# One set of split weights for both parts of an expert, and six experts in the order of their counts

## The chip, the cores and the metric

The kernel runs on one core of a Trainium2 chip. The metric is the device time of one execution in microseconds, as a median of the runs. TensorE is called PE here, VectorE DVE, ScalarE ACT, GpSimd POOL and SyncE SP, as in the profile.

## The reference

```
# q, k, v, a_re, a_im: (4, 8, 768, 48); S_re, S_im start at zero
for t in range(768):                       # gated linear attention
    S_re, S_im = ar*S_re - ai*S_im + k_t v_t^T, ar*S_im + ai*S_re
    y[t] = q_t @ S_re
x = y as (3072, 384)
noisy = x @ w_gate + log1p(exp(x @ w_noise)) * noise     # 8 experts
top2, softmax over the two
out[r] = sum over the two of  wt * (relu(x[r] @ w1[e]) @ w2[e])   # 384x1024, 1024x384
h = max(max(out @ u1, out @ u2), out @ u3)               # 384x768
return h @ w_out                                         # 768x384
```

With 3072 tokens and two experts each, 6144 rows fall on eight experts: 768 on average, and the counts are known only when the kernel runs.

## The kernel before

The work has four stages. **Attention**: 24 chunks of 128 tokens, four batches of six chunks. The k-th chunks of the four batches make a level, so there are six levels, and the state (`mb`) of each batch goes from level to level: it is added to (L777) and multiplied by the decay `lx` (L783). `chunk` (L695) and `gates` (L456) write the steps of a chunk. **Routing**: `route` (L822) takes two chunks at a time, twelve times in all. It finds the two experts of each token and the row that the token gets in each (PE's L882 to L886, DVE's L866 to L900), and `scatter` (L937, issued by POOL, L940) writes the token's row, split into two f16 halves, into `xs_rows`, where each expert has its own 3072 rows. **Experts**: relu(x w1) w2 with every operand split into two f16 halves, so that three matmuls stand for one. **Final stage**: `hidden` and `last` (L1541 to L1586) gather the two results of each token from `ys_rows` and compute the three products, their maximum and the last product.

An expert is computed in two parts. `first_pass(e)` takes its first 384 rows (RA), `second_pass(n)` the next 432 (RB), 816 in all (CAP). Rows beyond that go through a loop behind the experts, which is skipped where no expert has that many. A part is: rows of `xs_rows` loaded with a transpose (L1006, six transfers), 72 matmuls into eight tiles of h (L1037, in the second pass L1098), relu and its low half on ACT and DVE (L437; L1046, L1107), 72 matmuls back (L1057, L1124; of 432 rows, 48 make a tile of their own in 24 short matmuls, L1131), eviction to `ya` (L443, L1144) and its writing to `ys_rows` (L1069, L1152). A first pass writes its rows to `yf_rows` as well.

`weigh` (L1008) brings an expert's weights: seven pieces, each loaded by SP into one of four buffers `wst` (L997), then split by ACT (high half, L985) and DVE (low half, L987). Each expert has its weights loaded and split for both passes, but for the expert that is last of the first passes and first of the second ones: 15 sets of 7 pieces.

`bump` sees to it that the first 384 rows of an expert are full before the attention's last chunks are routed; the first passes thus need only the rows routed by then. `weigh_u` prepares the weights of the final stage: 15 pieces `raw`, three operations of DVE each into `ua` (L1177, L1182, L1186) and a split.

All steps up to the final stage are recorded as operations with their dependences, tiles and a key (place, name); a planner lists them engine by engine as the program is built, with a table of numbers by name, `P["o"]`, that sets which comes first. Each engine then runs its list in that order. Ten or so names in the table belong to the experts: `xw`, `xx`, `x1`, `xe`, `x2`, `xo` for first passes, the ones with y for second passes. SP issues nearly all transfers, in order, so a transfer that waits holds those behind it.

Of the kernel before, what the change touches and what calls it, by code (L numbers as in the profile page):

```python
# [35 lines left out]
    o=dict(load=-278.44, e1=-80.82, g=-44.76, ex=27.33, lam=13.6, t1=124.93, t2=491.73, f=-344.44, sin=58.57,  # L36
           tc=-621.27, qkv=204.29, v=669.22, a0=-227.64, a=84.82, b=-227.33, d=-609.19, c=-58.23, s=-165.23,
           l=90.33, f_=14.8, rt=-247.65, scat=-246.48, zf=803.51, gate=-153.95, noise=149.71, xw=125.96, xx=-312.17,
           x1=-201.57, xe=-424.5, x2=17.72, xo=-1189.75, yw=61.09, yx=-118.02, y1=-594.47, ye=185.57, y2=-134.08,
           yo=454.95, uw=1011.11, ue=388.46, pl=276.27, z=-83.6, mr=971.2),  # L40
# [208 lines left out]
def tile_kernel(ctx, tc, q, k, v, a_re, a_im, w_gate, w_noise, noise, w1, w2,  # L249
# [20 lines left out]

    xs = nc.dram_tensor("xs_rows", (E * NT, 2 * HD), F16).ap()

    NX = -(-((E - 2) * RA - (E * CAP - 2 * NT)) // 128) * 128
# [5 lines left out]
    zs = nc.dram_tensor("z_rows", (NT, 2 * HD), F16).ap()  # L279

# [93 lines left out]
    more = const.tile([128, E], F32, name="more")  # L374
# [630 lines left out]
    def load_rows(e, t, lo, hi, j):  # L1005
        return nc.sync.dma_start_transpose(t[:, j, :hi - lo], xs[e * NT + lo:e * NT + hi, j * 128:(j + 1) * 128])  # L1006
# [10 lines left out]
    def first_pass(e):  # L1017
        def pr(x):
            return NA + 1.5 * e, x

        weigh(e, "w1", "w2", e, pr("xw"), [("sl", ends[GA - 2], None)])
        for k in range(KD):
            for z in range(2):
                def f_x(e_, j=z * KD + k):
                    ins = load_rows(e, tl("xa", e), 0, RA, j)
                    for o in later:
                        tc.declare_no_dep(ins.ins, o.ins, reason="the second pass's rows begin after the first's")
                    loads.append(ins)
                load(f_x, pr("xx"), [("xa", e, (k, z))], xfer=0.65,
                     r=[("xs", i, None) for i in range(NA)], row="xa")  # L1030
        for f in range(KF):
            b = ("g", (e, 1, f))
# [599 lines left out]
```

## Time and profile before

| | us |
|---|---|
| median of 3 runs (978.99 to 984.77) | 984.25 |
| profiled execution: span from the first to the last instruction | 983.5 |
| PE busy (95%) | 930.6 |
| PE's weight loads busy (60%) | 586.8 |
| DVE busy (58%) | 574.0 |
| ACT busy (48%) | 476.0 |
| POOL busy (14%) | 139.0 |

The profile gives no time of that execution outside its span, so sums are made against the span. Its mean granted clock on PE is 0.979 of full speed. The transfers move 150.98 MB. A share is a mean over stages that differ: the stretches show which engine is full where.

### The profile page before, as it was taken

How to read it: one execution, taken by the hardware profiler on the slowest of the kernel's cores; microseconds unless marked ns; L12 is line 12 of the kernel's file. 1: busy time of each engine (PE TensorE's matmuls, PEld its weight loads, DVE VectorE, ACT ScalarE, POOL GpSimd, SP SyncE). 2: the span in 40 equal slices, each digit the busy share in tenths (PEclk: the TensorE clock that was granted, in tenths of full speed). 3: DMA queues.
4: the chain of work that ended last, by engine and by line, in shares of the span. 5: the costliest groups of instructions: out<-in, count | busy, mean ns of one | idle time of the engine just before them, and what ended most of it. 6: DMA issues, size and time to landing. Idle time of an engine off the chain costs nothing. (4 is left out here: it accounts for less than half of the span.)

```text
span 983.5 us, 16814 instructions
## 1 busy us (share of the span) xinstructions
PE 930.6 (95%) x6312; PEld 586.8 (60%) x6312; DVE 574.0 (58%) x1252; ACT 476.0 (48%) x922; POOL 139.0 (14%) x197
## 2 busy tenths in 40 slices
PE   3989778899999999899999999999799999999998
PEld 1868667787666766455555555555675445454544
DVE  5989748999655756565887764454344332424231
ACT  7998748978644556243445444333233132313221
POOL 0101442422001000520100000000433030300000
PEclk9999969999999999899999999999999999999999
DMA  9999848796765546379888785552335141502000
GB/s 150 211 214 271 195 120 159 182 194 165 191 185 168 158 153 201 123 223 312 253 253 238 209 208 155 147 141 79 107 116 142 40 133 36 140 25 78 25 9 33
DMA packets 247902, 150.98 MB, mean 154 GB/s; under 512 B 196488, under 2 KB 235528, under 8 KB 247816
## 3 DMA queue, kind: packets, MB, share of 16 engines
q1 hardware_dynamic: 241672, 130.98, 52.1%
q0 software_dynamic: 6144, 18.88, 6.4%
q8 instruction: 50, 0.82, 0.4%
q14 instruction: 36, 0.29, 0.1%
HBM read 89.78 MB, written 45.81 MB: 138 GB/s over the span
## 5 line engine op out<-in xcount | busy, mean ns | idle before, releaser
L437 ACT ACTIVATE hh<-bk 128x384 f16<-128x384 f32 (+1 forms) x128 | 64.6, 508 | 85.4 <-PE bk L1098 43.2
L985 ACT ACTIVATE w<-wst 128x768 f16<-128x768 f32 (+1 forms) x77 | 71.1, 932 | 59.6 <-PE bk L1057 23.3
L1057 PE MATMUL bk<-w,hh 128*128 128x384 f16 x576 | 98.6, 331 | 1.3 <-issue 1.3
L1037 PE MATMUL bk<-xa,w 128*128 128x384 f16 x576 | 99.6, 326 | 0.0
L987 DVE SCALAR_TENSOR_TENSOR w<-wst,w 128x768 f16<-128x768 f32 (+1 forms) x77 | 81.4, 1068 | 12.4 <-ACT w L985 11.5
L1571 ACT ACTIVATE th<-mx 128x512 f16<-128x512 f32 (+1 forms) x42 | 23.8, 568 | 127.2 <-DVE mx L1570 125.5
L1057 PEld LDWEIGHTS <-hh 128*128 128x128 f16 x576 | 56.7, 99 | 41.6 <-issue 6.5
L1124 PEld LDWEIGHTS <-hh 128*128 128x128 f16 x576 | 55.0, 98 | 40.3 <-issue 5.0
L1037 PEld LDWEIGHTS <-w 128*128 128x128 f16 x576 | 55.1, 98 | 34.4 <-issue 1.4
L1569 DVE TENSOR_TENSOR mx<-mx,u 128x512 f32<-128x512 f32 (+1 forms) x42 | 25.6, 610 | 62.5 <-PE u L1557 62.5
L1507 POOL DMA_INDIRECT yg<-ys_rows,sy x42 | 43.5, 1036 | 119.6 <-ACT za L1511 104.4
L940 POOL DMA_INDIRECT xs_rows<-xhl,sl x48 | 55.4, 1154 | 35.5 <-issue 18.5
L443 DVE COPY ya<-bk 128x384 f32<-128x384 f32 x37 | 20.6, 558 | 67.7 <-PE bk L1057 45.7
L732 PE MATMUL sc<-qt,kt 96*128 96x128 f32 x384 | 55.4, 287 | 4.5 <-issue 1.8
L732 PEld LDWEIGHTS sc<-qt,kt 96*128 96x128 f32 x384 | 49.3, 197 | 12.1 <-issue 4.1
L1098 PE MATMUL bk<-xa,w1b 128*128 128x432 f16 x288 | 53.2, 346 | 0.0
L1098 PE MATMUL bk<-xa,w 128*128 128x432 f16 x288 | 53.2, 346 | 0.0
L1107 DVE SCALAR_TENSOR_TENSOR hh<-bk,hh 128x432 f16<-128x432 f32 x64 | 37.9, 605 | 24.9 <-ACT hh L437 24.8
L1124 PE MATMUL bk<-w2b,hh 128*128 128x384 f16 x288 | 48.4, 326 | 0.0
L1124 PE MATMUL bk<-w,hh 128*128 128x384 f16 x288 | 48.4, 326 | 0.0
L1570 DVE TENSOR_TENSOR mx<-mx,u 128x512 f32<-128x512 f32 (+1 forms) x42 | 25.7, 611 | 37.4 <-PE u L1557 33.2
L1513 DVE SCALAR_TENSOR_TENSOR z<-yg,wt,za 128x384 f32<-128x384 f32 x22 | 12.8, 614 | 58.7 <-ACT za L1511 52.2
(204 smaller groups left out, 2012.7 us busy)
## 6 DMA issues: line engine op xcount, KB each, us to landing
wst<-in_moe_w_dram SPq DMA_DIRECT2D x45, 512.0 KB
wst<-in_moe_w_dram SPq DMA_DIRECT2D x60, 384.0 KB
xs_rows<-wst SPq DMA_DIRECT2D x8, 1152.0 KB
ys_rows<-ya SPq DMA_DIRECT2D x48, 192.0 KB
raw<-in_moe_w_dram SPq DMA_DIRECT2D x9, 768.0 KB
ar<-in_a_re_dram SPq DMA_DIRECT2D x24, 192.0 KB
ai<-in_a_im_dram SPq DMA_DIRECT2D x24, 192.0 KB
q<-in_q_dram SPq DMA_DIRECT2D x24, 192.0 KB
```

What stands on the lines that cost most here:

```text
L437: nc.scalar.activation(o, i, f, **kw)
L732: nc.tensor.matmul(tl("sc", (i, g))[:, j, :], tl("kt", i)[:, h, :], tl("qt", i)[:, h, :], start=True, stop=True)
L940: ins = nc.gpsimd.indirect_dma_start(out=xs, out_offset=bass.IndirectOffsetOnAxis(ap=sl[:, i, t:t + 1], axis=0), in_=tl("xhl", i), in_offs ...
L985: nc.scalar.activation(hi, src, AF.Copy, scale=scale)
L987: nc.vector.scalar_tensor_tensor(lo, src, scale, hi, op0=OP.mult, op1=OP.subtract)
L1037: nc.tensor.matmul(tl(*b)[:, :RA], tl("w1", e)[:, w, k, f * 128:(f + 1) * 128], tl("xa", e)[:, x + k, :RA], start=(k == m == 0), stop=(k = ...
L1057: nc.tensor.matmul(tl(*b)[:, :HD], tl("hh", e)[:, a, f, t * 128:(t + 1) * 128], tl("w2", e)[:, w, f], start=(f == m == 0), stop=(f == KF - ...
L1098: nc.tensor.matmul(tl(*b)[:, :RB], tl(n1, inst)[:, w, k, f * 128:(f + 1) * 128], tl("xa", xi)[:, x + k], start=(k == m == 0), stop=(k == K ...
L1107: nc.vector.scalar_tensor_tensor(tl("hh", xi)[:, 1, f], tl(*b)[:, :RB], 0.0, tl("hh", xi)[:, 0, f], op0=OP.max, op1=OP.subtract)
L1124: nc.tensor.matmul(tl(*b)[:, :HD], tl("hh", xi)[:, a, f, ts_], tl(n2, inst)[:, w, f], start=(f == m == 0), stop=(f == KF - 1 and m == 2))
L1507: nc.gpsimd.indirect_dma_start(out=y, out_offset=None, in_=src, in_offset=bass.IndirectOffsetOnAxis(ap=row[:, i, s:s + 1], axis=0))
L1570: nc.vector.tensor_tensor(a, a, ps[2], op=OP.max)
```

## The change

- The functions `first_pass` and `second_pass` become one, `expert(n, part, at, fresh)`. Only experts 0 and 1 have an early part (NF = 2), which takes rows from the chunks routed early; `bump` fills their first 384 rows alone.
- The parts come in a fixed order: expert 0's first, expert 1's first and second, then both parts of each of six experts one after the other, then expert 0's second. Weights are loaded and split once for both parts, but twice for expert 0: 9 sets of 7 pieces.
- The six are not experts 2 to 7 by number but by rank of their counts. DVE computes the ranks after the last route (`p_1`), SP loads the six numbers into registers (`p_er`), and the transfers of weights and rows take the expert from a register (`of`). The row limits by rank are 816, 784 and four times 768; a part of 400 or 432 rows has a tile of 16 or 48 rows, one of 384 has none. The loop for rows beyond takes the limit of each expert.
- Rows that a lower limit leaves unwritten are written once (`f_n`), fewer rows of zeros are needed, and the table `P["o"]` is a new one in all its numbers, so that the order on every engine changes.

```
-    o=dict(load=-278.44, e1=-80.82, g=-44.76, ex=27.33, lam=13.6, t1=124.93, t2=491.73, f=-344.44, sin=58.57,
...
+    o=dict(a=1637.24, a0=879.39, b=-18448.79, c=-886.02, d=-34103.66, e1=-2857.66, er=1057.34, ex=4707.9, f=-2809.26,
...
+    NF = 2
+    CAPS = [CAP] * NF + [816, 784, 768, 768, 768, 768]
...
+    xs3, ys3, yf3 = (x.rearrange("(e r) d -> e r d", e=E) for x in (xs, ys[:E * CAP], yf))
+    ER = {}
+    def of(n):
+        return slice(n, n + 1) if n < NF else bass.ds(ER[n], 1)
...
-                                         src[e][k * 128:(k + n) * 128].rearrange("(k p) f -> p k f", p=128))
+                                         src[of(e), k * 128:(k + n) * 128].rearrange("o (k p) f -> p (o k) f", p=128))
...
-    def first_pass(e):
+    def expert(n, part, at, fresh):
+        lo = RA * part
+        rows = CAPS[n] - RA if part else RA
+        early = n < NF and not part
+        inst = (n, part) if fresh else (n, 0)
...
+        if fresh:
+            weigh(n, n1, n2, inst, (NA + 1.5 * at, "xw") if early else (NI + at, "yw"),
+                  [("sl", ends[GA - 2], None)] if early else ([("er", n, None)] if n >= NF else []) + ([("swap", 0, None)] if swapped else []))
...
+            load(lambda e_, f_o=f_o: f_o(e_, ys3), pr("xo"), [("ys", xi, t)], xfer=0.6, r=[y + (None,)])
+            if part and t == nt - 1 and CAPS[n] < CAP:
+                def f_n(e_, y=y):
+                    nc.sync.dma_start(ys3[of(n), CAPS[n]:].rearrange("o n d -> (o n) d"), tl(*y)[:CAP - CAPS[n]])
+                load(f_n, pr("xo"), [("ys", xi, "no")], xfer=0.3, r=[y + (None,)])
+            if not part:
+                load(lambda e_, f_o=f_o: f_o(e_, yf3), pr("xo"), [("yf", n, t)], xfer=0.6, r=[y + (None,)])
...
+            key, rank, c2 = Q["key"], Q["rank"], Q["ohr"].rearrange("p (a b) -> p a b", b=E)
+            nc.vector.scalar_tensor_tensor(key, cnt, float(2 * E), iota8, op0=OP.mult, op1=OP.subtract)
+            nc.vector.memset(key[:, 0:NF], -1.0)
...
+        def p_er(n):
+            def f(e_):
+                ER[n] = nc.values_load(Q["ordi"][0:1, n - NF:n - NF + 1], engines=[mybir.EngineType.SP], min_val=0, max_val=E - 1,
...
-    for e in range(E):
-        first_pass(e)
...
-    for n in range(E):
-        second_pass(n)
...
+    parts = [(0, 0, True), (1, 0, True), (1, 1, False)] + [(n, part, not part) for n in range(NF, E) for part in range(2)] + [(0, 1, True)]
+    for at, (n, part, fresh) in enumerate(parts):
+        expert(n, part, at, fresh)
```

The new table moves steps of the attention too. The first place is PE at the last of the twelve routes. Before (`w_1952` is an expert's w1, seventh of eight first passes):

```order
L1037 MATMUL bk_249<-xa_2146,w_1952 128x384
L882 LDWEIGHTS tri_103
L882 MATMUL ps_389<-a_139,tri_103 128x16
L886 LDWEIGHTS ones_105
L886 MATMUL ps_389<-acc,ones_105 128x8
```

After (`w_2699` is expert 0's w2, `hh_2906` its h; the rows of the route have other lines):

```order
L1091 MATMUL bk_227<-w_2699,hh_2906 128x384
L892 LDWEIGHTS tri_103
L892 MATMUL ps_389<-a_139,tri_103 128x16
L896 LDWEIGHTS ones_105
L896 MATMUL ps_389<-acc,ones_105 128x8
```

What stays behind the route is the rest of the same part, then whole parts; what stood ahead of it changes from more than six first passes to one half of one.

The second place is POOL at the first scatters, which wait in turn for a route; `mb_113` to `mb_116` are the four batches' states. Before, twelve scatters (each with its spacer) stand in a row from the last row here on:

```order
L783 TENSOR_TENSOR mb_115<-mb_115,lx_801 96x8x48
L783 TENSOR_TENSOR mb_116<-mb_116,lx_801 96x8x48
L870 TENSOR_TENSOR acc<-acc,a_139 128x8 x4
L783 TENSOR_TENSOR mb_114<-mb_114,lx_1292 96x8x48
L939 MEMSET spacer 1x1
L940 DMA xs_rows<-xhl_501,sl 24576x768
```

After:

```order
L949 MEMSET spacer 1x1
L950 DMA xs_rows<-xhl_601,sl 24576x768
L949 MEMSET spacer 1x1
L950 DMA xs_rows<-xhl_601,sl 24576x768
L793 TENSOR_TENSOR mb_114<-mb_114,lx_1286 96x8x48
L793 TENSOR_TENSOR mb_115<-mb_115,lx_1286 96x8x48
L793 TENSOR_TENSOR mb_116<-mb_116,lx_1286 96x8x48
L949 MEMSET spacer 1x1
L950 DMA xs_rows<-xhl_640,sl 24576x768
L949 MEMSET spacer 1x1
L950 DMA xs_rows<-xhl_640,sl 24576x768
```

The decays of three states now stand behind the fourth scatter; eight scatters follow them. In all, the 20 decays stand on POOL, where before 11 did and 9 on DVE.

The third place is SP after the last route. Before, in a second pass (weights `wst`, rows `xa`, results `ya`):

```order
L1006 DMA_TRANSPOSE xa_2544<-xs_rows 128x432
L997 DMA wst_1803<-in_moe_w_dram 128x1024
L1174 DMA raw_4809<-in_moe_w_dram 128x1536
L1006 DMA_TRANSPOSE xa_2544<-xs_rows 128x432
L997 DMA wst_1853<-in_moe_w_dram 128x2x384
L1006 DMA_TRANSPOSE xa_2544<-xs_rows 128x432
```

After, where the registers and the first weights of the first expert by rank stand:

```order
L1429 DMA ys_rows<-wst_2402 128x3x384
L1261 TENSOR_LOAD ordi
L1016 DMA_TRANSPOSE xa_2583<-xs_rows 128x432
L1007 ISA
L1007 DMA wst_160<-in_moe_w_dram 128x1024
L1261 TENSOR_LOAD ordi x4
L1016 DMA_TRANSPOSE xa_2583<-xs_rows 128x432
L1261 TENSOR_LOAD ordi
L1148 DMA raw_3608<-in_moe_w_dram 128x1536
L1007 ISA
L1007 DMA wst_2279<-in_moe_w_dram 128x1024
```

Each transfer whose expert is in a register has one more instruction (ISA) ahead of it; the transposes of expert 1's second part (`xa_2583`) stand between.

## Rows read from the trace of the kernel before

**Rows 1.** Stretches: us, busy us (instructions) of PE, PEld, DVE, ACT, POOL, PEclk, DMA, GB/s.

```profile
62.00:104.00 42.00, 39.43 (x399) 34.25 (x398) 36.56 (x111) 37.78 (x86) 5.81 (x9) 0.96 1.08 236
104.00:163.00 59.00, 47.98 (x400) 40.01 (x400) 39.29 (x123) 39.06 (x88) 22.65 (x38) 0.83 0.65 153
163.00:205.00 42.00, 35.88 (x349) 31.08 (x348) 41.22 (x112) 38.72 (x83) 17.96 (x20) 0.96 0.79 179
...
432.00:687.00 255.00, 255.00 (x1576) 142.86 (x1575) 159.74 (x237) 105.49 (x167) 10.08 (x14) 1.00 0.68 199
```

**Rows 2.** PE in order of time (start us, us, line, what, count) at three places.

```profile
207.37 1.15 PE L1037 MATMUL bk<-xa,w 128*128 128x384 f16 x6
...
431.68 0.17 PE L882 MATMUL ps<-a,tri 128*128 128x16 f16 x1 [0.86 <-DVE a L866]
...
688.81 0.39 PE L1557 MATMUL u<-ua,u1h 128*128 128x256 f16 x2 [0.65 <-DVE ya L443]
```

**Rows 3.** PE in order of time, 445 to 512 us.

```profile
445.94 11.86 PE L1037 MATMUL bk<-xa,w 128*128 128x384 f16 x72
457.64 12.01 PE L1057 MATMUL bk<-w,hh 128*128 128x384 f16 x72
469.49 13.30 PE L1098 MATMUL bk<-xa,w 128*128 128x432 f16 x72
482.73 1.16 PE L1131 MATMUL bk<-w,hh 128*48 128x384 f16 x12
...
496.72 13.30 PE L1098 MATMUL bk<-xa,w1b 128*128 128x432 f16 x72
```

**Rows 4.** DVE by line; then the spread of two lines (min/median/max ns, first and last start).

```profile
L987 DVE SCALAR_TENSOR_TENSOR w<-wst,w 128x768 f16<-128x768 f32 (+1 forms) x77 | 81.4, 1068 | 12.4 <-ACT w L985 11.5
...
L783 DVE TENSOR_TENSOR mb<-mb,lx 96x384 f32<-96x384 f32 x9 | 6.9, 772 | 0.0
...
L1182 DVE SCALAR_TENSOR_TENSOR ua<-raw,ua x15: 541/950/960, 452.1 to 573.5; 128x768 int32<-128x768 int32 x9, 128x384 int32<-128x384 int32 x6
...
L783 POOL TENSOR_TENSOR mb<-mb,lx x11: 839/856/3901, 68.9 to 304.4; 96x384 f32<-96x384 f32 x11
```

**Rows 5.** DVE in order of time: the first L649 of a level.

```profile
62.35 0.55 DVE L649 SCALAR_TENSOR_TENSOR tn<-tn,bk 128x384 f32<-128x384 f32 x1
...
103.81 0.55 DVE L649 SCALAR_TENSOR_TENSOR tn<-tn,bk 128x384 f32<-128x384 f32 x1
...
161.82 0.55 DVE L649 SCALAR_TENSOR_TENSOR tn<-tn,bk 128x384 f32<-128x384 f32 x1
...
205.34 0.55 DVE L649 SCALAR_TENSOR_TENSOR tn<-tn,bk 128x384 f32<-128x384 f32 x1 [0.22 <-ACT tn L437]
```

**Rows 6.** POOL, DVE and PE in order of time, around the scatters.

```profile
109.55 3.90 POOL L783 TENSOR_TENSOR mb<-mb,lx 96x384 f32<-96x384 f32 x1 [11.61 <-DVE lx L613]
...
114.96 1.16 POOL L940 DMA_INDIRECT xs_rows<-xhl,sl  x1 [1.48 <-issue]
...
129.46 0.96 POOL L940 DMA_INDIRECT xs_rows<-xhl,sl  x1 [0.22 <-issue]
...
122.30 0.34 PE L753 MATMUL py<-qt,mb 96*64 96x128 f32 x2 [1.08 <-issue]
...
132.48 0.55 DVE L777 TENSOR_TENSOR mb<-mb,ps 96x384 f32<-96x384 f32 x1 [8.84 <-remote]
...
405.34 0.27 PE L753 MATMUL py<-qt,mb 96*64 96x128 f32 x1 [1.10 <-issue]
```

**Rows 7.** The tile nbi (min/median/max ns); then SP's queue in order of time.

```profile
L1444 SPq TENSOR_LOAD <-nbi x1: 538/538/538, 689.7 to 689.7; - x1
...
494.00 0.43 SPq L997 DMA_DIRECT2D wst<-in_moe_w_dram  x1
...
499.74 1.12 SPq L1006 DMA_TRANSPOSE xa<-xs_rows  x1
```

**Rows 8.** SP's queue, 250 to 690 us: line, waited for, us in total, times, longest.

```profile
SPq L1152 <- DVE ya L1144: 62.9, 8, 18.4
```

More of the change, by code (lines that the diff above doesn't have):

```diff
@@ L373, in tile_kernel @@
     nc.vector.tensor_scalar(first, pidx, 0.0, None, op0=OP.is_equal)
-    more = const.tile([128, E], F32, name="more")
+    more = const.tile([128, NF], F32, name="more")
     wt = const.tile([128, NI, 2], F32, name="wt")
@@ L1024, in f_x @@
                 def f_x(e_, j=z * KD + k):
[L1025 to L1030, printed above, removed]
+                    ins = load_rows(n, tl("xa", xi), lo, lo + rows, j)
+                    if early:
+                        for o in later:
+                            tc.declare_no_dep(ins.ins, o.ins, reason="the second part's rows begin after the first's")
+                        loads.append(ins)
+                load(f_x, pr("xx"), [("xa", xi, (k, z))], xfer=0.75 if rows > RA else 0.65,
+                     r=[("xs", i, None) for i in range(NA if early else NI)] + ([("er", n, None)] if n >= NF else []), row="xa")
         for f in range(KF):
-            b = ("g", (e, 1, f))
+            b = ("g", (n, 1 + 2 * part, f))
             prev = None
@@ L1036, in f_1 @@
                     for m, (w, x) in enumerate(((0, 0), (0, KD), (1, 0))):
-                        nc.tensor.matmul(tl(*b)[:, :RA], tl("w1", e)[:, w, k, f * 128:(f + 1) * 128],
-                                         tl("xa", e)[:, x + k, :RA], start=(k == m == 0), stop=(k == KD - 1 and m == 2))
-                prev = O.add(f_1, {"PE": 0.49}, pr("x1"), r=[("w1", e, (k, 0)), ("w1", e, (k, 1)), ("xa", e, (k, 0)), ("xa", e, (k, 1))],
-                             w=[b + (k,)], hold=[("hh", e), ("vg",) + b[1:]], prev=prev)
+                        nc.tensor.matmul(tl(*b)[:, :rows], tl(n1, inst)[:, w, k, f * 128:(f + 1) * 128],
+                                         tl("xa", xi)[:, x + k, :rows], start=(k == m == 0), stop=(k == KD - 1 and m == 2))
@@ L1117, in second_pass @@
+            O.add(f_h, en(["act"], rows, True), pr("xe"), r=[b + (None,)], w=[("hh", xi, (f, 0))], hold=slots(b))
+            O.add(f_l, en(["dve"], rows), pr("xe"), r=[b + (None,), ("hh", xi, (f, 0))], w=[("hh", xi, (f, 1))], hold=slots(b))
+        nt, nr = divmod(rows, 128)
+        assert nr <= 64
+        for t in ([nt] if nr else []) + list(range(nt)):
+            b = ("g", (n, 2 + 2 * part, t))
+            prev = None
             ts_ = slice(t * 128, t * 128 + (nr if t == nt else 128))
@@ L1211, in f_4 @@
         def f_4(e_):
-            nc.vector.tensor_tensor(acc[:, GA + 1], acc[:, GA], more, op=OP.add)
+            nc.vector.tensor_copy(acc[:, GA + 1], acc[:, GA])
+            nc.vector.tensor_tensor(acc[:, GA + 1, :NF], acc[:, GA, :NF], more, op=OP.add)
         pr = (NA, "rt")
@@ L1216, in bump @@
         O.add(f_3, {"DVE": 0.08}, pr, r=[("more", 0, 0)], w=[("more", 0, 1)])
-        O.add(f_4, {"DVE": 0.08}, pr, r=[("more", 0, 1), ("acc", GA, None)], w=[("acc", GA + 1, None)], two=True)
+        O.add(f_4, {"DVE": 0.16}, pr, r=[("more", 0, 1), ("acc", GA, None)], w=[("acc", GA + 1, None)], two=True)
     NB = 52
@@ L1236, in swap @@
         Q["nbi"] = rt.tile([128, 1], I32, name="nbi")
+        Q["ordi"] = rt.tile([128, E], I32, name="ordi")
     def prefix(dst, src):
```

158 lines of the change are left out of this document (67 added, 91 removed).

## The prediction

> **What bounds the kernel now.** I read the busy times stage by stage first, then the order of TensorE's (PE's) matmuls, then the engines that make it wait, last the transfers. The stages [rows 1] show two regimes. From 432 to 687 us PE is busy 255.00 us of 255: the second parts of the experts come without a gap, and every matmul taken out there is time. Between 62 and 205 us (levels of the attention) no engine is full, VectorE (DVE) and ScalarE (ACT) come nearest (41.22 and 38.72 us of 42 from 163 to 205), and PE, 35.88 us busy, is not. From 207 us on matmuls of the first passes fill PE's gaps [rows 2], and PE is the engine that is full again. So the kernel before runs three levels at the pace of DVE and ACT, then from 207 to 688 us at PE's, with the rest of the attention strewn between the first passes. The final stage begins at 688.81 us [rows 2], 294.7 us before the end of the span (983.5 us). The change does not touch its code, so it is carried over as a constant.
>
> **Sizes on PE.** One first pass is 469.49 - 445.94 = 23.55 us, by twice its first half (72 matmuls of 384 columns: 457.64 - 445.94 = 11.70 us) 23.4; one second pass is 496.72 - 469.49 = 27.23 us, of which 72 matmuls of 432 columns take 13.24 (469.49 to 482.73) and the half tile's two groups 2 x 1.09 = 2.19, the rest 11.7 [rows 3]. A part of 384 rows thus costs 23.4 us whichever part it is; one of 400 rows, between the two, about 12.2 + 11.7 + 2.2 = 26.1 us.
>
> **What it removes.** Four experts lose the 48 rows above 768: 4 x (27.23 - 23.4) = 15.3 us, the one with limit 784 loses 1.1: 16.4 us of PE work, all in the stretch where PE is full. Six of fifteen sets of split weights go (42 pieces of 105, with their loads; a piece is about 1.07 us of DVE [rows 4]): some 45 us of DVE work, but it lay beside a PE that was full, so by itself it is worth nothing. It would count only where DVE binds.
>
> **What it moves** is the greater part. The early passes shrink from eight to two, so the attention's last levels no longer compete with 187 us of first passes for PE: 81 matmuls of expert 0 (13 us) stand in PE's order ahead of the last route's, where before more than six passes stood. After the last route all that is left is expert work in one row: 63 matmuls of expert 0 (10.2), expert 1's two parts (23.4 + 27.2), the six sorted ones (50.6 + 49.5 + 4 x 46.8 = 287.3) and expert 0's second part (27.2), 375.4 us in all. The time is therefore T + 375.4 + waits + 294.7, with T the start of the last route's matmul on PE. Before, T is 431.68 us, and what is left then is 15 + 72 matmuls (14.1), one first pass and eight second ones: 255.4 us, which is where the 688 comes from [rows 2]. Break-even, with no wait, is T = 688.2 - 375.4 = 312.8 us.
>
> *T.* Levels begin at 62.35, 103.81, 161.82, 205.34 us by the marks on DVE [rows 5]: periods of 41.5, 58.0 and 43.5. The 58.0 holds the stall below, of 14 to 17 us. From 62.35, five levels at these undisturbed paces are 41.5 + 4 x 43.5 = 215.5, so the last level's work is done near 278 (the route of a level's last chunks falls at its end, and in the last level nothing of a next one is in the way). Nine of the state's decays (mb, line 783) leave DVE for GpSimd (POOL): 9 x 0.77 = 6.9 us less on DVE over the six levels, of which I take 3: T = 275 with no stall.
>
> *The moved decays.* What they cost on POOL has two ends: 0.86 us, the median, and 3.90 us, the one at 109.55 us, while DVE ran one tensor operation after the other [rows 4, 6]. Four in a row at the worst are 15.6 us per level of 42 on an engine that is 14 to 43% busy in these levels [rows 1], and each is needed only by its batch's chunk of the next level; so 0, and at most 3 us per level if a route's scatters queue ahead of them. The Trainium skill, "SBUF — State Buffer", section "Who interferes with whom", says that a DVE operation with two SBUF inputs contends with a GpSimd instruction that reads SBUF. The 3.90 against 0.86 us agrees. The rule speaks against the move. What it gives from rows: if all nine took 3.90 us in line, 9 x 3.04 = 27 us would be added over the levels, T would be 302 and the time 977; that case is counted with rival A.
>
> *Stall 1.* From 114.96 to 130.42 us POOL scatters twelve times back to back, about 1.3 us apart. From the sixth on PE has a gap of about 1.1 us for nearly each (as at 122.30), in which it waits for nothing that the profile shows, and DVE stands for 8.84 us, until 132.48 [rows 6]; PE's mean granted clock in that stage is 0.83 against 0.96 beside it. From 163 to 205 us, where the scatters come in fours between other work, DVE is at 41.22 of 42 [rows 1]. So it is the row of twelve that costs. In the new order four scatters come, then three decays, then eight scatters: undone wholly that saves about 15, undone not at all 0. Eight are nearer to twelve than to four, but the gaps began only at the sixth; I take 8 saved, so 7 are added. *Stall 2*, around 405 us with the same kind of gap [rows 6], fell under twelve scatters in a row too; the new last level has eight: 0 to 8, I take 4. T = 286; bounds 275 to 298.
>
> *Waits after T.* DVE has then the preparation of the final stage's weights (15 pieces of three operations, two of them 0.95 us as a median [rows 4], and a split), which before lay spread from 450 to 575 us beside the second passes. In the new order it is packed into four parts: adding its rows at the mean durations gives 14.0, 24.4, 23.8 and 25.9 us of DVE for 23.4, 27.2, 23.4 and 27.2 us of PE. Nearly full is not over: 0 to 8 us, I take 3.
>
> *The registers.* Sorting adds nine DVE operations on at most 64 columns (one or two us in all), six loads of a register on SP (0.54 us, the load of the block count on the same engine [rows 7]), and ahead of every transfer with a register one more instruction on SP. The chain is: last matmul of expert 0, eviction and two splits on DVE, sorting, load, then expert 2's weights. It has all of expert 1 (50.6 us) as cover, for about 14 issues of 0.4 to 1.2 us [rows 7]: nothing. Uncovered it would cost some 20 us. The writing of two parts' rows with registers waits for the write before it; such writes are a tile (3.9 us) apart on PE, so I take 0 here too. *Small ones*: the final stage's first transposes now stand after the last part: 1 us.
>
> Sum: 286 + 375.4 + 3 + 1 + 294.7 = 960 of span, 23 less than the 983.5 of the profiled execution, which is itself within a microsecond of the median (984.25). Forecast **961 us**.
>
> **The rivals.**
> *A, T is late* (no change): the attention doesn't run freely, because PE's busy share from 62 to 104 us (39.43 of 42 [rows 1]) is real need. Then 13 us of filler come on top, stalls 1 and 2 stay (15 + 8): T = 275 + 36 = 311 and the time 985. Against it: from 207 to 432 us 224 us hold about 150 us of first passes, leaving 74 for two levels with stall 2, so a level needs some 33 us of PE. Between the forecast and A lie times of 973 to 985, reached by part of A or by slow decays.
> *B, SP becomes the bound* (slower). Per sorted expert SP issues 7 weight pieces, 12 transposes of 1.12 us and 10 row writes: 17 x 0.43 + 12 x 1.12 = 21 us [rows 7], plus 29 instructions for the register. At 0.1 us these make 24, at a register load's 0.54 us 37, against 46.8 on PE. If besides each write holds SP until the one before has landed (half a tile of PE, 2 us, for want of a row, for eight of them) it is 53, and transposes and weights behind them on the same queue come late: 6 us an expert, 37 in all: 997. It decides from 47 us of SP per expert. For it: SP waited 62.9 us for one kind of eviction in the second passes [rows 8], with loads queued behind it. Against it: all three conditions are needed.
> *C, the limits don't hold*: a ranked expert above its limit sends the rest to the loop behind the experts, with its 3.1 MB of weights loaded again, 16 us at the 199 GB/s of the last stretch [rows 1], and its products after that: 25 to 30 us, 990. By the reference's draw the six counts are 804, 774, 762, 757, 755, 731 under limits of 816, 784 and 768: the loop stays out unless another draw is used.
> *D, both stalls vanish* and DVE keeps up: 286 - 11, no 3: 947.
>
> **How the numbers follow.** Forecast (950 to 972) 0.60, A and what lies towards it (973 to 988) 0.20, B 0.09, C 0.03, D 0.08. Runs of before differ by 5.8 us, so about 1% (9.8 us) is what can be told from no change. Faster by over 1% holds the forecast, D and a quarter of A: 0.73. Within 1%: 0.14. Slower: B, C and a little of A: 0.13. Range 945 to 988.
>
> **What would show it.** Right: the last route's matmul near 286 us (275 to 298); first parts of experts 0 and 1 at 23.4 us, four of the six ranked experts at 46.8; no gap on PE longer than 2 us from there to the final stage; final stage 295 us; DVE above 90% busy for 100 us after the last route. Wrong: levels longer than 46 us with POOL or DVE as releaser, or PE without a gap in them (A); PE waiting for weights or rows with SP without a pause (B); PE idle between expert 1 and the first ranked one (the registers); the loop's matmuls (C). If T is near 286 and the time is not, it is one of the waits behind it that I set at 3 or 0.

## The result

The changed kernel takes 974.09 us as a median of 4 runs (972.02 to 975.36) against 983.50 (978.99 to 984.77) of the kernel before beside it: a ratio of 0.9905, 95% interval 0.9879 to 0.9931. It is faster by 9.4 us, where 961 had been forecast, 23 less. The profiled execution has a span of 972.0 us. All kernels were run in groups, each group with runs of the kernel before on the same chip; in two of the six groups told of here the kernel before itself took 957 us, so times are compared within a group only.

PE of the changed kernel in order of time, as in [rows 2] and [rows 3]: the last route (L892), expert 1's first part (L1065 its first product, L1091 its second), the first ranked expert, one of the 768-row experts, the last transposes and the start of the final stage (L1564):

```profile
294.24 0.17 PE L892 MATMUL ps<-a,tri 128*128 128x16 f16 x1
...
304.59 11.86 PE L1065 MATMUL bk<-xa,w 128*128 128x384 f16 x72
317.37 2.92 PE L1091 MATMUL bk<-w,hh 128*128 128x384 f16 x17 [0.91 <-DVE hh L1075]
...
332.88 12.39 PE L1065 MATMUL bk<-xa,w 128*128 128x432 f16 x67
...
410.74 3.25 PE L1065 MATMUL bk<-xa,w 128*128 128x384 f16 x19
414.45 8.77 PE L1065 MATMUL bk<-xa,w 128*128 128x384 f16 x53 [0.46 <-DMA xa<-xs_rows]
423.06 7.15 PE L1091 MATMUL bk<-w,hh 128*128 128x384 f16 x43
...
484.41 11.86 PE L1065 MATMUL bk<-xa,w1b 128*128 128x384 f16 x72
...
507.81 2.44 PE L1065 MATMUL bk<-xa,w 128*128 128x384 f16 x14
...
675.65 0.60 PE L1379 MATMUL bk<-ident,raw 128*128 128x128 f32 x4
677.30 0.38 PE L1564 MATMUL u<-ua,u1h 128*128 128x256 f16 x2 [1.04 <-DVE ua L1385]
```

The last route stands at T = 294.24 us; 286 had been taken. From there to the final stage it is 677.30 - 294.24 = 383.06 us, where the sum had 375.4 of work and 4 of waits; from there to the end of the span 972.0 - 677.3 = 294.7, as before to the tenth. So of the 12 us by which the span misses the 960 of the sum, 8.2 lie ahead of the last route and 3.7 behind it. (Times are some 1.9 us longer than spans in every run, where the forecast had allowed 1.)

Sizes of the parts hold: 507.81 - 484.41 = 23.40 us for one of 384 rows. Expert 1's first part is the exception: 332.88 - 304.59 = 28.29 us. In it PE waits for `hh` four times, 2.4 us in all, and the slower second product stands in the time behind those gaps. The other losses behind T are the rows of the first ranked expert (0.46 us, and 12.32 us instead of 11.70 for that product) and the transposes ahead of the final stage with their wait (677.30 - 675.65 = 1.65 us).

Stretches of the changed kernel from one level mark on DVE to the next, the last one up to T; the columns are those of [rows 1]:

```profile
63.29:103.25 39.96, 37.89 (x390) 32.41 (x389) 36.95 (x108) 36.03 (x83) 8.10 (x9) 0.99 1.07 237
103.25:150.43 47.18, 41.31 (x370) 35.71 (x369) 38.39 (x112) 36.33 (x80) 24.43 (x32) 0.89 0.81 179
150.43:191.80 41.37, 39.77 (x426) 34.50 (x423) 38.91 (x114) 37.09 (x84) 12.44 (x16) 1.00 0.59 110
191.80:242.64 50.84, 44.41 (x408) 37.30 (x407) 40.47 (x124) 42.06 (x90) 14.82 (x24) 0.90 0.56 137
242.64:294.24 51.60, 43.53 (x398) 33.82 (x396) 37.49 (x142) 28.92 (x63) 27.59 (x48) 0.93 0.50 145
```

The first of them takes 40 us and the third 41.4; the second, fourth and fifth take 47, 51 and 52, with PE's mean granted clock at 0.89 to 0.93. What these three have in common, and the others not, shows on POOL, in order of time:

```profile
121.42 0.96 POOL L950 DMA_INDIRECT xs_rows<-xhl,sl  x1 [0.22 <-issue]
122.40 2.43 POOL L793 TENSOR_TENSOR mb<-mb,lx 96x384 f32<-96x384 f32 x3
...
251.98 1.63 POOL L950 DMA_INDIRECT xs_rows<-xhl,sl  x1 [0.22 <-issue]
253.63 2.45 POOL L793 TENSOR_TENSOR mb<-mb,lx 96x384 f32<-96x384 f32 x3
...
262.99 1.06 POOL L950 DMA_INDIRECT xs_rows<-xhl,sl  x1 [6.89 <-DVE slf L907]
...
272.59 0.96 POOL L950 DMA_INDIRECT xs_rows<-xhl,sl  x1 [0.22 <-issue]
```

In each of the three levels a batch of four scatters (L950) stands ahead of three decays (L793), and in two of them eight scatters in a row follow. At the end of the second row of eight, DVE, ACT and PE in order of time:

```profile
270.77 0.29 DVE L805 TENSOR_REDUCE zp<-bk 128x16 f32<-128x128 f32 x1 [2.68 <-remote]
...
274.40 0.69 DVE L746 TENSOR_TENSOR pm<-sc,mask 128x512 f32<-128x512 f32 x1 [2.60 <-remote]
...
275.14 0.49 ACT L451 ACTIVATE xhl<-bk 128x384 f16<-128x384 f32 x1 [5.23 <-remote]
...
275.15 0.44 PE L760 MATMUL py<-pm,vb 128*64 128x128 f32 x4 [3.93 <-DVE pm L746]
```

DVE and ACT stand for 2.6 and 5.2 us with a releaser that the profile can't name, and PE waits 3.9 us for DVE. The clock behind that, in stretches of 4 us:

```profile
272.00:276.00 4.00, 0.85 (x12) 0.85 (x14) 1.03 (x5) 0.49 (x1) 1.33 (x3) 0.95 0.91 362
276.00:280.00 4.00, 3.47 (x26) 2.94 (x23) 3.73 (x25) 1.41 (x6) 0.42 (x3) 0.50 0.34 96
```

PE is busy 0.85 us of 4, and in the stretch after that it has 0.50 of its clock (1.2 GHz, the lower of its two levels). So a stop costs PE its own length and, in the next 4 us, half its speed.

### The profile page after: what moved, and what is told of

It reads as the page before. It is cut to its first block, busy times and chain, and to the rows that moved or that the text cites. A ratio compares the mean times of both kernels' runs of the same rounds, so it can differ in the third digit from the quotient of the medians.

```text
span 972.0 us, 16761 instructions
## 1 busy us (share of the span) xinstructions
PE 917.1 (94%) x6216; PEld 584.3 (60%) x6216; DVE 530.2 (55%) x1218; ACT 438.1 (45%) x874; POOL 150.2 (15%) x204
## 5 line engine op out<-in xcount | busy, mean ns | idle before, releaser
L1091 PEld LDWEIGHTS <-hh 128*128 128x128 f16 x1152 | 112.2, 98 | 80.4 <-issue 5.4
L447 ACT ACTIVATE hh<-bk 128x384 f16<-128x384 f32 (+2 forms) x128 | 63.4, 497 | 157.2 <-PE bk L1065 155.1
L1065 PE MATMUL bk<-xa,w 128*128 128x384 f16 (+2 forms) x648 | 112.3, 331 | 0.5 <-DMA xa<-xs_rows 0.5
L1091 PE MATMUL bk<-w,hh 128*128 128x384 f16 x648 | 109.6, 329 | 2.4 <-DVE hh L1075 2.4
L1075 DVE SCALAR_TENSOR_TENSOR hh<-bk,hh 128x384 f16<-128x384 f32 (+2 forms) x128 | 71.1, 565 | 69.7 <-ACT hh L447 69.7
L1065 PEld LDWEIGHTS <-w 128*128 128x128 f16 x648 | 63.0, 98 | 42.9 <-issue 1.4
L1065 PE MATMUL bk<-xa,w1b 128*128 128x384 f16 (+1 forms) x504 | 85.9, 332 | 0.0
L1091 PE MATMUL bk<-w2b,hh 128*128 128x384 f16 x504 | 83.4, 326 | 0.0
L1065 PEld LDWEIGHTS <-w1b 128*128 128x128 f16 x504 | 49.3, 98 | 35.3
L1514 POOL DMA_INDIRECT yg<-ys_rows,sy x42 | 43.5, 1036 | 120.6 <-ACT za L1518 107.0
L950 POOL DMA_INDIRECT xs_rows<-xhl,sl x48 | 55.7, 1161 | 29.5 <-issue 10.5
L1590 PE MATMUL o<-woh,th 128*128 128x384 f16 x144 | 46.9, 326 | 0.0
L1590 PE MATMUL o<-wol,th 128*128 128x384 f16 x144 | 46.9, 326 | 0.0
L1590 PE MATMUL o<-woh,tl 128*128 128x384 f16 x144 | 46.9, 326 | 0.0
```

What stands on the lines that cost most here:

```text
L447: nc.scalar.activation(o, i, f, **kw)
L950: ins = nc.gpsimd.indirect_dma_start(out=xs, out_offset=bass.IndirectOffsetOnAxis(ap=sl[:, i, t:t + 1], axis=0), in_=tl("xhl", i), in_offs ...
L1065: nc.tensor.matmul(tl(*b)[:, :rows], tl(n1, inst)[:, w, k, f * 128:(f + 1) * 128], tl("xa", xi)[:, x + k, :rows], start=(k == m == 0), sto ...
L1075: nc.vector.scalar_tensor_tensor(tl("hh", xi)[:, 1, f, :rows], tl(*b)[:, :rows], 0.0, tl("hh", xi)[:, 0, f, :rows], op0=OP.max, op1=OP.sub ...
L1091: nc.tensor.matmul(tl(*b)[:, :HD], tl("hh", xi)[:, a, f, ts_], tl(n2, inst)[:, w, f], start=(f == m == 0), stop=(f == KF - 1 and m == 2))
L1514: nc.gpsimd.indirect_dma_start(out=y, out_offset=None, in_=src, in_offset=bass.IndirectOffsetOnAxis(ap=row[:, i, s:s + 1], axis=0))
```

## Experiments

T is the start of the last route's first matmul on PE, "rest" the time from T to the first matmul of the final stage, both of the profiled execution; the time is the median. Groups are in the order in which they ran.

| group | kernel | T | rest | time | before beside it | ratio (95%) |
|---|---|---|---|---|---|---|
| 1 | the changed kernel | 294.24 | 383.06 | 974.09 | 983.50 | 0.9905 (0.9879 to 0.9931) |
| 2 | e1_no_scatter | 272.94 | 380.03 | 949.09 | 985.15 | 0.9648 (0.9611 to 0.9685) |
| 2 | e2_spaced | 284.27 | 392.91 | 978.39 | 985.15 | 0.9940 (0.9918 to 0.9962) |
| 2 | e3_fixed_order | 299.65 | 381.48 | 975.46 | 985.15 | 0.9902 (0.9874 to 0.9931) |
| 2 | e4_less_u | 298.75 | 382.45 | 973.62 | 985.15 | 0.9889 (0.9854 to 0.9925) |
| 3 | e8_spaced_early | 282.92 | 381.14 | 961.31 | 983.71 | 0.9786 (0.9748 to 0.9824) |
| 3 | e9_u_held | 291.41 | 386.71 | 978.98 | 983.71 | 0.9949 (0.9919 to 0.9980) |
| 3 | e10_both | 288.71 | 387.81 | 968.12 | 983.71 | 0.9837 (0.9797 to 0.9878) |
| 3 | e6_new_table_on_before | 307.53 | 434.84 | 1034.26 | 983.71 | 1.0509 (1.0455 to 1.0563) |
| 4 | e7_limits_816 | 281.79 | 397.66 | 961.43 | 956.96 | 1.0047 (1.0020 to 1.0073) |
| 4 | e5_old_table | 316.76 | 384.45 | 988.91 | 956.96 | 1.0299 (1.0250 to 1.0349) |
| 4 | e11_before_spaced | 420.12 | 257.01 | 968.06 | 956.96 | 1.0108 (1.0072 to 1.0145) |
| 4 | e12_decays_dve | 273.19 | 382.30 | 944.35 | 956.96 | 0.9865 (0.9826 to 0.9905) |
| 5 | e13_after_again | 280.32 | 381.07 | 948.76 | 956.77 | 0.9902 (0.9872 to 0.9932) |
| 5 | e14_before_again | 405.73 | 257.10 | 956.73 | 956.77 | 0.9999 (0.9981 to 1.0016) |
| 5 | e15_decays_dve_again | 273.32 | 381.23 | 943.30 | 956.77 | 0.9854 (0.9834 to 0.9874) |
| 5 | e16_spaced_early_again | 280.14 | 383.49 | 951.36 | 956.77 | 0.9930 (0.9908 to 0.9953) |
| 6 | e17_dve_and_spaced | 286.48 | 381.56 | 962.92 | 983.71 | 0.9759 (0.9715 to 0.9803) |
| 6 | e18_decays_dve_third | 298.03 | 382.59 | 973.42 | 983.71 | 0.9876 (0.9840 to 0.9911) |

The theory after the first trace (S): rows of scatters stop the other engines, PE's clock falls behind each stop, and that makes T late. The rival (P): the chain of work in a level is longer than I had read it.

**The scatters left out.**

```
         def scatter(i, t):
             def f(e_):
                 nc.gpsimd.memset(spacer, 0.0)
-                ins = nc.gpsimd.indirect_dma_start(
...
-                scats.append(ins)
```

> All 48 scatters of token rows are left out (the one-element memset ahead of each stays), so the experts compute on rows that hold no token; the order on every other engine is that of the changed kernel. Theory S (the rows of scatters stop DVE and ACT, PE's granted clock falls behind each stop, and that is most of the 19 us by which the last route, at 294.2 us, is later than the 275 without stalls): last route at 275 to 280 us, time 955 to 960. Theory P (the levels' own chain of work is longer than read, scatters cost little): last route at 288 or later, time 968 to 974.

PE's last route in this kernel:

```profile
272.94 0.17 PE L892 MATMUL ps<-a,tri 128*128 128x16 f16 x1
```

T is 272.94 us, 21 earlier, and the time 949, earlier than either theory said. Theory P falls: with no scatter the levels take 41, 40, 41, 45 and 43 us. Theory S stands so far, but leaving the scatters out takes away whatever else they cost as well, so e1 can't say that it is their rate. T is within 2 us of the 275 that the prediction took "with no stall".

**Scatters further apart.**

```
-                scats.append(ins)
+                scats.append(ins), [nc.gpsimd.memset(spacer, 0.0) for _ in range(8)]
```

> Eight one-element memsets more behind each scatter on POOL, so that scatters come about 2.2 us apart instead of 1.27. Theory S, if the rate of the scatters is what stops the others: last route at 280 to 286, time 962 to 967. Theory S, if their number is: no change, 974. Theory P: 974 to 980, since the scatters end later and the decays behind them too.

T comes 10 us earlier, the time doesn't: rest is 392.9. The 978.39 lies where theory P had put it; the profiled execution, with T at 284, is the fastest of nine (972.32), so time and T are not of the same one, and e8 below is the better test. PE in order of time behind T:

```profile
287.77 0.17 PE L896 MATMUL ps<-acc,ones 128*128 128x8 f16 x1 [3.33 <-POOL spacer L949]
```

PE waits for POOL, where the running counts (L880) stand behind the last, slowed scatters (3.3 us here, and 2.9 us once more at 298.67). Up to T no wait with an unnamed releaser is left on DVE or ACT. So the rate of the scatters matters, and the end of the scatters is a path of its own. Hence the next kernel, spaced for the first 16 chunks only (`range(8 if i < 16 else 0)`):

> The eight memsets behind a scatter only for the first 16 of the 24 chunks; the last 16 scatters, on whose end PE and expert 1's second part wait, come as fast as in the changed kernel. Theory S by rate (fast rows of eight stop DVE and ACT; late scatters cost by their lateness): last route at 280 to 287 us, what follows it 383 us as in the changed kernel, time 962 to 968. Rival (spacing itself only moves the loss): 974 to 978.

T 282.9, rest 381.1, 961.31 us: 2.1% faster than the kernel before (interval 1.8 to 2.5), the changed kernel 0.95%, in another group. Behind its last scatters, 1.3 us apart, one stop is left, on DVE and ACT:

```profile
275.24 0.17 DVE L899 TENSOR_TENSOR rw<-ps,basee 128x16 f32<-128x16 f32 x1 [5.94 <-remote]
```

In group 5, where the kernel before took 957 us, the same kernel did nothing for T:

> The early scatters spaced, beside the changed kernel. Theory S: where the stalls are there, 10 to 14 us faster than the changed kernel; where they are not, no gain or up to 8 us slower (spacing only makes accumulating counts wait on POOL).

It took 951.36 against 948.76 of the changed kernel, 0.9930 against 0.9902 with intervals that overlap: no gain, as S had it. On the kernel before, spacing (group 4) cost 11 us, since T moved from some 406 (measured in group 5) to 420:

> The kernel before with eight more one-element memsets behind each scatter of the first 16 chunks. Theory S by rate: the stall behind the twelve scatters at 115 to 130 us (some 15 us) goes in this kernel too: fourth level mark at 148 to 152 us, time 968 to 974. Rival (before, the time is set by PE's sum from 207 us on, and what is won earlier is lost there): 980 to 985.

Neither theory had that price; that 968 lies in the range named for S is chance, since that was meant beside 984. Spacing is not a remedy where the stops are absent.

**Registers taken out.**

```
-        return slice(n, n + 1) if n < NF else bass.ds(ER[n], 1)
+        return (lambda e: slice(e, e + 1))([0, 1, 4, 2, 5, 3, 6, 7][n])
```

> The six experts' numbers are constants (the order that the counts of this draw give), so there is no register load and no extra instruction ahead of a transfer; DVE still computes the ranks. My prediction (registers are hidden): 974, within 2 us. Rival (SP's register work delays weights or rows): 964 to 969.

975.46 us, and a rest 1.6 us shorter: the registers are hidden, and with them the part of rival B (SP the bound) that rested on them falls.

**Less work on DVE behind the last route** (two of three operations per piece left out).

> Two of the three DVE operations that prepare each piece of the final stage's weights are left out (30 operations, about 24 us of DVE), so the final weights are wrong. Theory (DVE is over-full behind the last route, and PE waits for it in expert 1's first part, 4.9 us): 969 to 970. Rival (that wait has another cause, as the routing work or the sorting ahead of it): 973 to 974.

No change: rest 382.45, and expert 1's first part still takes 28.28 us. The reading "DVE over-full" falls. The orders of ACT and DVE show the cause. In the changed kernel, ACT, where 5 evictions of h are done and three are to come:

```profile
312.11 0.49 ACT L447 ACTIVATE hh<-bk 128x384 f16<-128x384 f32 x1 [0.97 <-PE bk L1065]
318.34 0.84 ACT L995 ACTIVATE u1h<-ua 128x768 f16<-128x768 f32 x1 [5.74 <-DMA wst<-in_moe_w_dram]
319.09 0.47 ACT L447 ACTIVATE hh<-bk 128x384 f16<-128x384 f32 x1
```

and DVE:

```profile
314.55 0.56 DVE L1151 TENSOR_SCALAR ua<-raw 128x768 int32<-128x768 int32 x1 [0.65 <-DMA raw<-in_moe_w_dram]
...
317.23 0.95 DVE L1160 SCALAR_TENSOR_TENSOR ua<-raw,ua 128x768 int32<-128x768 int32 x1
```

ACT stands 5.7 us at the high half of a final-stage weight (`u1h`, L995). The profile names a transfer of `wst` as the releaser; the time fits the last `ua` operation on DVE (317.23 + 0.95 = 318.18), whose first one had itself waited for a transfer of `raw`. The evictions of h, ready on PE, are queued behind it. With the two operations out, ACT:

```profile
320.15 0.84 ACT L995 ACTIVATE u1h<-ua 128x768 f16<-128x768 f32 x1 [3.04 <-DVE ua L1151]
...
327.89 1.06 ACT L995 ACTIVATE w1b<-wst 128x1024 f16<-128x1024 f32 x1 [3.20 <-DMA wst<-in_moe_w_dram]
```

The first wait ends earlier after the part's start (309.12 on PE; 320.15 is 11.0 us on, before 13.8), and the splits of the next weights, which wait for their own transfers, take its place. That these are held back was the point of the next kernel:

```
-            load(g_0, pr("uw"), [raw + (None,)], xfer=cols * 0.0028, r=[("swap", 0, None)], row="raw")
+            load(g_0, pr("uw"), [raw + (None,)], xfer=cols * 0.0028, r=[("swap", 0, None), ("ys", (1, 0), 2)], row="raw")
```

> The loads of the final stage's weights wait until expert 1's first part has been written, so their preparation stands no more among that part's evictions. Theory W (PE waits in expert 1's first part because evictions of h stand behind steps that wait for a transfer, in the orders of ACT and DVE): from the last route to the final stage 378 to 380 us instead of 383.1, time 970 to 971. Rival (the wait comes from the routing and sorting work on DVE): 383, and 974.

PE:

```profile
301.77 11.86 PE L1065 MATMUL bk<-xa,w 128*128 128x384 f16 x72
...
327.06 13.30 PE L1065 MATMUL bk<-xa,w 128*128 128x432 f16 x72
...
387.36 10.42 PE L1065 MATMUL bk<-xa,w1b 128*128 128x432 f16 x47 [4.94 <-DMA xa<-xs_rows]
```

Expert 1's first part is 327.06 - 301.77 = 25.29 us, 3.0 of the 4.9 us less: for these, theory W is borne out, though both its numbers were missed (rest 378 to 380, time 970 to 971). What the other 1.9 us are stays open. In the new order PE waits 4.9 us for the rows of the first ranked expert's second part, and the rest is 3.6 us longer than in the changed kernel. With the spacing too it is 968:

> The edits of the two kernels before it together: if they add, 958 to 965; if the spacing only moves the loss, 970 to 975.

They don't add: 6.8 us worse than the spacing alone.

**The limits by rank taken back** (`CAPS = [CAP] * E`).

> All row limits 816, so five ranked experts have a part of 432 rows again; everything up to the last route is in the same order. My sum: 16.4 us more of PE behind the last route, time 990 to 991. Rival (the rows cut lay beside other waits): 974 to 982.

Start of the final stage, with T at 281.79:

```profile
679.45 0.38 PE L1564 MATMUL u<-ua,u1h 128*128 128x256 f16 x2 [1.04 <-DVE ua L1385]
```

Rest 397.66, against 381.07 of the changed kernel in group 5: 16.6 us, in the slowest of its ten executions. The PE work removed was sized right (16.4). By the ratios of the two groups it is 1.0047 - 0.9902, 1.45% of 957, 13.9 us: most or all of it counts.

**The two halves of the change apart.** The changed kernel with the old table:

> The changed kernel with the table of numbers of the kernel before (and the one new name): 288 expert matmuls, both early parts whole, stand ahead of the last route. If the order is worth little beside the sharing and the limits (the expert work alone counts, 16.4 us of PE less than before): 965 to 975. If the new order is needed to use the sharing: 985 or more.

3.0% slower than the kernel before. T is 316.76 although the levels up to the fourth are as fast (148 and 196 us for the fourth and fifth marks), and behind it PE's waits are led by

```profile
PE bk L1065 <- DMA xa<-xs_rows: 26.0, 7, 9.4
```

for rows that come too late. The kernel before with the new table:

> The kernel before with the changed kernel's table of numbers alone: weights still split for each pass, all eight first passes, no limits by rank. By my sum (PE work taken out 16.4 us, the rest is the attention run ahead of the experts): last route near 294 us, then 111 instead of 81 matmuls done, 16.4 us more of expert work than the changed kernel, and DVE and ACT with 42 splits more behind the last route: 988 to 1000, slower than before. Rival (the table brings the gain, the sharing nothing): 970 to 978.

5.1% slower, 1034 us where 988 to 1000 had been expected; behind the last route PE waits for rows, and for splits of weights that the sharing would have made unneeded:

```profile
PE bk L1098 <- DMA xa<-xs_rows: 8.4, 5, 3.1
PE bk L1037 <- ACT w L985: 8.3, 3, 4.6
```

Sharing without the new order loses, the new order without sharing loses; together they gain 1%. The two are from different groups, but each ratio is clear of 1 by 2.5% or more. Neither table was written for the other program, so these two runs say that the parts depend on one another, not what a table fitted to each would give.

**The decays on DVE.**

```
-                EN[e].tensor_tensor(m, m, tl("lx", s)[:, :, js:js + 1].to_broadcast([D2, H, D]), op=OP.mult)
+                nc.vector.tensor_tensor(m, m, tl("lx", s)[:, :, js:js + 1].to_broadcast([D2, H, D]), op=OP.mult)
```

> All 20 decays of the state are issued on DVE, at the same places of the order. My prediction's view (decays on POOL take work off a full DVE and cost nothing there): 20 x 0.77 = 15 us more of DVE over six levels, of which some 5 to 8 show: 978 to 982. Rival (the contention rule: decays on POOL are held up behind scatters and DVE's own operations): 966 to 974.

944.35 us, but beside a kernel before of 957: not to be read against the 974. So the group was run again with the changed kernel in it.

> The changed kernel once more, as the measure for the others of this group. Theory S (stops behind fast rows of scatters make the last route late, and they depend on more than the kernel): where the kernel before takes about 984, 974 with the last route at 292 to 300; where it takes about 957, 943 to 947 with the last route at 272 to 277. Rival (the changed kernel's late route has nothing to do with what makes the kernel before slow): 974 in both.

> The kernel before once more, for its trace beside the others. Theory S: at 984 DVE stands for more than 5 us behind the twelve scatters (fourth level mark near 162, 58 us after the third); at 957 it doesn't (near 147), and the last route is some 20 us earlier than 431.7.

> The 20 decays on DVE, beside the changed kernel. If the decays on POOL cost or save nothing that shows: within 2 us of the changed kernel's time in this group. My prediction's view (POOL takes work off a full DVE): 4 to 8 us slower than it. Rival (contention, and decays queued behind scatters): 4 to 10 us faster.

T is 273.3 against 280.3 and the time 943.3 against 948.8: the nine moved decays, which were to save 3 us, are among twenty that cost 7 in this group. The 280.3 is also later than the 272 to 277 that theory S had named, so S leaves something out. What they do on POOL shows in the second level. DVE, POOL and PE of the changed kernel there (e13), and PE's clock behind it:

```profile
119.98 3.82 DVE L523 TENSOR_TENSOR tn<-ai,iv 128x384 f32<-128x384 f32 x2
...
120.92 2.45 POOL L793 TENSOR_TENSOR mb<-mb,lx 96x384 f32<-96x384 f32 x3
...
126.54 1.92 PE L742 MATMUL sc<-qt,kt 96*128 96x128 f32 x8 [2.79 <-DVE pm L746]
...
128.00:136.00 8.00, 8.00 (x73) 7.66 (x72) 5.43 (x15) 4.55 (x11) 4.96 (x8) 0.66 0.28 84
```

The same two multiplications of DVE and the same decays in e16, where the spacing brings the decays 4.6 us later, and the spread of the decays on DVE (e15):

```profile
120.68 1.05 DVE L523 TENSOR_TENSOR tn<-ai,iv 128x384 f32<-128x384 f32 x2
...
125.56 2.45 POOL L793 TENSOR_TENSOR mb<-mb,lx 96x384 f32<-96x384 f32 x3
...
L793 DVE TENSOR_TENSOR mb<-mb,lx x20: 544/545/549, 72.5 to 248.1; 96x384 f32<-96x384 f32 x20
```

Two multiplications that take 1.05 us take 3.82 while three decays run on POOL; PE waits 2.8 us for DVE behind them and has 0.66 of its clock in the stretch that follows. That level takes 45.5 us in e13 (e7 repeats both, 3.81 and 45.4), 41.0 with the decays on DVE, and 40.5 in e16, where the decays stand behind the same four scatters, spaced wider. So the queue ahead of the decays doesn't cost it; DVE being held while they run does: 4.5 of the 7 us. In the result's execution the pair held is another (L535 at 122.39 us: 3.34 us for 1.01). Of the rest, 2 us lie in the level from 62 us, which varies by more than that between executions with the decays on POOL (40.0 to 44.1), and 1.7 in the last level, where one multiplication took 2.46 us instead of 0.55 beside three decays. In e1 the three decays came elsewhere; there they took 3.65 us instead of 2.45 and DVE's pair 1.02, so it can be either engine that is held. On DVE a decay takes 545 ns; the 772 of [rows 4] is a mean, of which the median is 548 and only the three beside a decay on POOL are longer (0.73, 1.19 and 1.75 us).

**Both together.**

> Decays on DVE and the early scatters spaced, together. Where the kernel before takes about 984: the spacing gave 13 us and the decays should give some 5 more, 954 to 958, last route at 276 to 281. Where it takes about 957: 944 to 950, no better than the decays alone.

> Decays on DVE alone. Where the kernel before takes about 984: if decays queued behind the scatters are the way by which the rows of scatters stop the engines, 955 to 960; if the stop is of another kind, 967 to 971, five less than the changed kernel. Where it takes about 957: 942 to 945.

Where the stops are there, decays on DVE alone change nothing that can be told (T 298, within what the order of the changed kernel gave in e3 and e4; the 973 lies above both expected ranges), and with the spacing 0.9759 against 0.9786 of the spacing alone, with intervals that overlap. T is 286.5, not the 276 to 281 expected: behind the last, unspaced scatters ACT still stands for 6.0 us until 277.23. The two causes don't add in this group.

**What differs between groups.** The kernel before, DVE, PE and the rest in two stretches of 4 us under its row of twelve scatters, in the execution of [rows 6] and in that of e14_before_again:

```profile
124.00:128.00 4.00, 2.25 (x8) 1.34 (x7) 0.00 (x0) 0.68 (x2) 3.31 (x8) 0.71 0.40 148
128.00:132.00 4.00, 1.80 (x5) 0.86 (x6) 0.00 (x0) 0.00 (x0) 2.10 (x4) 0.50 0.41 150
```

```profile
124.00:128.00 4.00, 4.00 (x58) 3.74 (x57) 3.98 (x14) 3.55 (x10) 3.33 (x7) 1.00 0.41 149
128.00:132.00 4.00, 4.00 (x37) 3.73 (x38) 4.00 (x9) 4.00 (x10) 3.57 (x5) 1.00 1.04 240
```

The columns are those of [rows 1]. The scatters come about as fast in both, every 1.3 and 1.4 us; in the first DVE does nothing for 8 us, in the second it is full. Its last route is then 26 us earlier (405.73).

Nor is the stop bound to scatters. Early in the final stage POOL issues ten gathers of rows in a row (L1514), 1.25 us apart. Behind them, PE of e1, which has no scatters (group 2), and of e13 (group 5), in the second 12 us of the stage:

```profile
669.05 0.94 POOL L1514 DMA_INDIRECT yg<-ys_rows,sy  x1 [0.30 <-issue]
...
664.97:676.97 12.00, 8.67 (x58) 6.03 (x56) 3.69 (x10) 2.12 (x7) 3.81 (x5) 0.86 0.30 89
```

```profile
673.39:685.39 12.00, 12.00 (x99) 9.47 (x98) 6.18 (x16) 3.79 (x11) 4.16 (x5) 1.00 0.33 94
```

The final stage, to the end of the span, takes 292.0 to 294.8 us in all profiled executions of groups 1, 2, 3 and 6, with the scatters as they are, spaced or left out, and 286.7 to 288.5 in all of groups 4 and 5. So 6 to 8 us of the 25 to 27 between the groups lie here, in code that the change doesn't touch.

One and the same chip gave (groups 5 and 6) 957 us for the kernel before in one group and 984 in another, so the chip is not the cause. What the engines wait for ("remote", "issue") the profile doesn't name; that it is open is said below.

## Why the prediction was wrong

*What bounds and what is moved.* The form was right: the time is T + work + waits + final stage, and the work held (375.4 us: all parts of 384 rows at 23.40, the rest by e7). The final stage was taken as a constant, 294.7. It is so within a group with stops, but it holds one of the stops itself: without them it is 287.2 (e13).

*T, the step that failed.* On a base of 275 it adds 0 for the moved decays and 11 for the stalls. Where nothing stops, the changed kernel's T is 280.3 (e13), 5.3 over that base; with the decays on DVE it is 273.3. With stops it is 294.2, 13.9 more, where "I take 8 saved, so 7 are added" and "I take 4" had made 11. Together that is the 8.2 us by which T is late. The split is of single executions in two groups, and e18 warns against taking it for the result's own group: where the stops are, T stays at 298 with the decays on DVE, while it is 272.9 with the scatters left out (e1). Read in groups with stops alone, the stalls were the term: 21 us for 11. Stretch by stretch against e13, the one with the first row of eight is 1.7 us longer (47.2 for 45.5), the one with the second 6.8 (51.6 for 44.8), and the one between, 191.8 to 242.6, with scatters in fours alone, 7.5 (50.8 for 43.3). The step had said that fours cost nothing; it took that from one level, 163 to 205 us, of one execution.

*The moved decays.* Wrong in sign: "so 0, and at most 3 us per level if a route's scatters queue ahead of them", and a saving of 3; measured, 7 us lost for all twenty where nothing else stops. The step priced decays that are held on POOL and a queue ahead of them, not DVE's own work being held while they run (3.82 us for 1.05). The Trainium skill's rule ("SBUF — State Buffer", "Who interferes with whom") was weighed for this place, and the trace agrees with it: the multiplications that were held have two inputs in SBUF. The price worked out beside it, T = 302, leaves the 11 us of stalls out; with them it would have been 313, and 988 us.

*Waits behind T.* 7.7 us for 4. The main one, 4.9 us in expert 1's first part, is at the place named, but the reason (DVE nearly full) was wrong: e4 takes 24 us of DVE away and leaves it, and DVE is busy 84% of the 100 us behind T, not over 90%. For 3.0 us it is the order: evictions of h stand on ACT behind steps that wait for a transfer (e9).

*Registers, limits.* Right: nothing (e3; the added instructions on SP take 0.03 to 0.05 us each, a register load 0.27 as a median), and 16.4 us against 16.6 or 13.9 (e7). The break-even uses 688.2 where the row has 688.81; nothing hangs on it.

*Rivals.* A was the nearest in its number (985, and 973 to 985 on the way to it), by the part of it that kept the stalls; its filler didn't come on top (e1: with the same matmuls ahead of the last route, T is 272.9). B and C didn't occur: PE's one wait for rows is 0.46 us, and the loop's matmuls don't appear. D's time, 947, is close to what the changed kernel takes where the stops are absent (948.8), but by luck: T is 5 us later than D had it, the final stage 7 shorter, and there the kernel before takes 957 as well.

So the gain of 23 us that had been forecast is not there in either kind of group: 9.4 us with stops, 8.0 without. By the times, the absence of stops gives 26.7 us to the kernel before and 25.3 to the changed one, so the change removes 1.4 us of them, where the step on stalls had it remove 12. By T alone, in single executions, the stops cost 26.0 us before (431.68 for 405.73) and 13.9 after, which would be the 12; the two don't agree, e14's profiled execution being the fastest of its ten, and how much of the stops the change removes stays open. What is shown is that the stops belong to both kernels and that the moved decays lose where they were to save. Put back, the decays bring 5.5 us (0.9854 against 0.9902, intervals that just meet), in groups without stops; the spaced scatters bring some 12 in groups with them (0.9786 against 0.9905, from two groups).

## What to carry to other kernels

A step moved to an idle engine can hold the engine that it left: compare the durations of what runs there beside it (here 3.82 us for 1.05) before counting the time that it frees. When steps that wait for transfers share an in-order engine with evictions, look at the order and not at the sum of busy time; taking work away there moved the wait to the next transfer (e4). A stall with a releaser that the profile can't name may not be the kernel's at all: run the unchanged kernel more than once, in groups apart, before a forecast is built on its absence.

## What was not expected of the hardware

- Rows of scatters by POOL (1.3 us apart) stop DVE, ACT and PE for up to 8.8 us in some groups and not at all in others, with the same program on the same chip, 984 against 957 us. Ten gathers by POOL 1.25 us apart do the same in the same groups, also in a kernel without scatters (e1: final stage 294.3 us, for 287.2 in e13). With the scatters 2.4 to 3 us apart no such wait is left up to T (e2). What is waited for stays open: since gathers do it too, it isn't the writes to `xs_rows` alone, but no run separates the fetch of instructions, the transfers themselves or something outside the core.
- Three decays on POOL held two multiplications of DVE for 2.8 us (e13), and PE had 0.66 of its clock behind that.
- A PE that was busy 0.85 us of 4 ran its next 4 us at 1.2 GHz. So the stops cost clock as well as time: PE's mean clock in the changed kernel is 0.979 with them and 0.991 without (e13).
